# Fewer weight parts in the first five blocks, and the rest tied to the feed-forward steps at 0.85 a step

## The chip, the cores and the metric

The kernel is one program on 1 core of a Trainium2 chip. The metric is the device time of one execution in microseconds (us). The kernel before takes 1225.81 us, the median of 3 runs (1225.13 to 1226.35).

## The reference, cut to what matters

Three layers follow each other: linear attention with an exponential feature map, a feed-forward layer with a token shift and a gate, and a second feed-forward layer with a short convolution. The change touches the preparation of the weights of the second one (`w_k`, `w_r`, `w_v`).

```python
def _attn_ref(q, k, v, w_phi):            # batch 8, 8 heads, 576 tokens, head size 64, 128 features
    def phi(x):
        proj = np.einsum('bhsd,df->bhsf', x, w_phi)
        proj = proj - np.max(np.abs(proj), axis=-1, keepdims=True)
        return np.concatenate([np.exp(proj), np.exp(-proj)], axis=-1)
    q_p, k_p = (phi(q), phi(k))
    kv = np.einsum('bhsf,bhsd->bhfd', k_p, v)
    z = np.sum(k_p, axis=2)
    num = np.einsum('bhsf,bhfd->bhsd', q_p, kv)
    den = np.einsum('bhsf,bhf->bhs', q_p, z)[..., None] + 1e-06
    return num / den

def _moe_ref(x, mu_k, mu_r, w_k, w_v, w_r):    # d_model 512, d_ff 1024
    xk = mu_k * x + (1.0 - mu_k) * x_prev       # x_prev: x one token earlier
    xr = mu_r * x + (1.0 - mu_r) * x_prev
    k = np.maximum(xk @ w_k, 0.0)
    v = k * k @ w_v
    r = 1.0 / (1.0 + np.exp(-(xr @ w_r)))
    return r * v
```

## The kernel before, in words

Heads are worked in 32 pairs `Pi` (8 batches of 4 pairs). `block(Pi)` is the attention of several pairs at once: it turns the centred projections of pair `Pi` (`turn`, tiles `pt`, then `qf` through ScalarE's exponential), projects the keys of pair `Pi+2` (`front`, tiles `p` and `pk`), the queries of pair `Pi+1` (`pq`), sums keys against values for pair `Pi+1` (`sums4`, tile `pkv`) and gives the results of pair `Pi` (`results`, tile `pn`, normalised into `xn` by VectorE). `column` transposes a finished `xn` (tile `px`), and ScalarE copies it into `xT`, the input of the feed-forward layer. TensorE runs in the order in which the code is written (`manual_schedule`); the order on VectorE and ScalarE is fixed at build time by the framework's scheduler, and each engine runs its list in order.

Every projection ends in VectorE: a maximum (`mx`) and a subtraction (`t`) for each tile. The PSUM tiles of the attention come from five rotating buffers (`psa`), so `pk` of one block can only start when VectorE has read the `pn` tiles of the block before, and from block 5 on the second `pk` tile follows ScalarE's copy of `px`.

The feed-forward layer `moe(u)` runs over 16 half batches `u`. From pair 4 (`MS`) on, `feed` puts its steps behind the blocks: 6 steps behind block 4, 6 behind block 5, 7 behind block 6, 9 behind block 7, then 10. A step is one output tile: for `u` = 0 steps 0 to 7 are `psk`, 8 and 9 `psr`, 10 and 12 `psv`, 14 and 15 `psr`, 16 and 18 `psv`; the odd ones between are the reads of `psv`. The half batch `u` = 0 multiplies by the unsplit weights, the later ones by a high and a low half.

The three weights come as 64-bit numbers in 20 parts of 512 columns: 8 of `wk`, 2 of `wr`, 4 of `wv`, 2 of `wr`, 4 of `wv`. The generator `step` (L171 to L186) moves one part on: SP loads `raw` (512 KB, three buffers); ScalarE makes `h` from the upper words; VectorE builds a 32-bit number in `h` with four instructions (two `TENSOR_SCALAR`, two `SCALAR_TENSOR_TENSOR` that also read `raw`); SP stores `h` into the weight's tile (`wkl`, `wrh`, `wvl`), and `ready` counts up. `tick` (L209) loads a new part and finishes the part that was loaded two ticks earlier, so on SP's queue the load of part n+3 stands right behind the store of part n, whose `raw` buffer it takes. `pre` gives ScalarE its instruction early.

A tick stands in three sorts of places: twice in every block from -1 to 6; at the fixed steps of the table `WAT` behind blocks 4, 5 and 6; and in `want`, in front of a feed-forward step of `u` = 0, until `ready` is 2 (`AHEAD`) above the number of parts that this step reads (`needs`). A step of `u` = 1 then splits the parts (`split`: a copy on ScalarE, tile `wkh`, and a subtraction on VectorE, `wkl<-wkl,wkh`).

Of the kernel before, what the change touches and what calls it, by code (L numbers as in the profile page):

```python
# [27 lines left out]

MS, SLOW, SR = 4, 8, {4: 6, 5: 6, 6: 7, 7: 9}

WAT = {4: (4, 10), 5: (3, 7, 11), 6: (3, 5, 7, 9)}
DS0 = 10
AHEAD = 2
HS = S // 2
V1 = D + 1

# [6 lines left out]
def fused_kernel(ctx: ExitStack, tc: tile.TileContext, qk, va, wphi, ones2, mu, wk, wv, wr, win, wout, cw, out):  # L43
# [33 lines left out]
    def f(x):  # L77
        return x.bitcast(F32)
# [78 lines left out]
    with ExitStack() as p1:  # L157
# [30 lines left out]
        def split(n=None):  # L188

            while n is None or cleft[0] < n:  # L190
                if half:
                    hs, ls = half.pop()
                    V.behind("tensor_tensor", ls, f(ls), f(hs), ALU.subtract)
                    cleft[0] += 1
                if whole and (n is None or cleft[0] < n):
                    half.append(whole.pop(0))
                    A.behind("copy", half[0][0], f(half[0][1]))
                if n is None or not half:
                    return

        under, ready, whole, half, cleft = [], [0], [], [], [0]

        def pre():

            if under and under[0][1] == 2 and not under[0][2]:
                next(under[0][0])
                under[0][2] = True

        def tick():  # L209
            pre()  # L210
            new = [wsteps.pop(0), 0, False] if wsteps else None
            if new:
                next(new[0])
            if under and under[0][1] == 2:
                next(under.pop(0)[0], None)
            if new:
                under.append(new)
            for x in under:
                x[1] += 1

        wsteps = [step(wk, wkh, wkl, o) for o in range(0, 4096, 512)]
        for h in range(2):
            for w in ((wr, wrh, wrl), (wv, wvh, wvl)):
                n = w[1].shape[1] // 2
# [13 lines left out]
        def load(Pi):  # L238

            b, p = divmod(Pi, NP)  # L240
            raw = pool.tile([P, W], F32, tag="x", bufs=3, name="rqk")
            if Pi == 0:
                for c in (slice(KC0, W), slice(0, KC0)):
                    SY.dma_start(raw[:, c], qk[b, p, :, c])
            else:
                (SY if Pi < 3 else G).dma_start(raw, qk[b, p])
            xk[Pi] = raw
# [86 lines left out]
        def column_end(xn, xt, px):  # L334
            T.transpose(px[:, :P], xn[:, 4], ident)

            def copies():
                for h in range(2):
                    r = slice(64 * h, 64 * h + 64)
                    A.copy(xt[r, 513:577], px[r, r])  # L340
            return copies
# [46 lines left out]
        def block(Pi):  # L388

            nq, nk = Pi + 1 < B * NP, Pi + 2 < B * NP  # L390
            if 0 <= Pi < B * NP - 3:
                load(Pi + 3)
            if Pi >= 0:
                if Pi > MS:
                    x = column(Pi - 1)
                qf, t1 = turn(Pi)
                pr = psa.tile([P, 512], F32, tag="at", name="pr")
                if Pi > MS:
                    copies = column_end(*x, pr)
                turn_end(qf, t1, pr)  # L400
                if Pi > MS:
                    copies()
            pre()
            if nk:
                tk = front(Pi + 2)
            if -1 <= Pi < 7:
                tick()
            if 1 <= Pi <= MS:
                x = column(Pi - 1)
                column_end(*x, psm.tile([P, 512], F32, tag="mm", name="pr"))()  # L410
            if nq:
                ts[Pi + 1] += centre4(rows4(Pi + 1, 0, "pq"), "tq")
                del xk[Pi + 1]
                sums4(Pi + 1)
            if Pi >= 0:
                results(Pi, qf)
            pre()
            if nk:
                features(Pi + 2, tk)
                if Pi + 2 > 1:  # L420
                    load_v(Pi + 2)
            if -1 <= Pi < 7:
                tick()

        def attention(Pi):
# [39 lines left out]

        done = [0]

        def want(n):

            while ready[0] < min(n + AHEAD, 20):  # L470
                tick()
            due[0] += 1

        due = [0]
        needs = [*range(1, 9), 9, 10, 12, 14, 15, 16, 18, 20]

        def moe(u):
            b, hf = divmod(u, 2)
# [5 lines left out]
                    T.matmul(ps, f(wl), xh, start=first, stop=last)  # L484

            def need(n):
                want(n)
                if u:
                    split(n)

            def soon():
                if u == 0 and due[0] < len(needs) and ready[0] < min(needs[due[0]] + AHEAD, 20):
                    pre()
            o = hf * HS
            for j in range(2):
# [78 lines left out]
        load_v(1)  # L574

        def extras(Pi, n):
            if n in WAT.get(Pi, ()):
                tick()
            if n + 1 in WAT.get(Pi, ()):
                pre()  # L580
            if Pi == 7 and n == 14:
                taps()
            if Pi >= DS0 and dsteps and n in (3, 11):
                dsteps[0] = dsteps[0][0](), dsteps[0][1]
            if Pi >= DS0 and dsteps and n in (4, 12):
                raw, step = dsteps.pop(0)
                step(raw)
# [177 lines left out]
```

## Time and profile before

| | |
|---|---|
| median of 3 runs | 1225.81 us |
| the profiled execution, its own time | 1225.83 us |
| span of its trace | 1224.0 us |
| outside the span | 1.83 us |
| TensorE busy | 1202.0 us, 98% |
| VectorE busy | 762.1 us, 62% |
| ScalarE busy | 696.7 us, 57% |
| granted TensorE clock | 1.00, the upper level (2.4 GHz) throughout |

The busy shares are means over the whole span. The weights' parts are moved in its first 122 us, where the shares are others; the rows further down show that stretch. The profiled execution took within 0.02 us of the median, so a sum made against it stands against the median as well.

### The profile page before, as it was taken

The numbers are of one execution on the slowest core, as the hardware profiler recorded it, in microseconds if no ns is written. First come the engines' busy times: TensorE is split into PE (matmuls) and PEld (weight loads), VectorE is DVE, ScalarE is ACT, GpSimd is POOL, SyncE is SP. The second block draws the span as 40 slices with busy tenths as digits, with TensorE's granted clock in tenths as the row PEclk, the third lists the DMA queues.
The fourth block names the chain that finished last, engine by engine and source line by source line (L and its number), as shares of the span: only waits on it lengthen the run. The fifth ranks groups of instructions, "written<-read, shape, count | busy, mean of one in ns | idle before, by whom it ended". The sixth has DMA issues, their size and how long they took to land.

```text
span 1224.0 us, 29034 instructions
## 1 busy us (share of the span) xinstructions
PE 1202.0 (98%) x11920; PEld 1135.5 (93%) x11920; DVE 762.1 (62%) x1584; ACT 696.7 (57%) x1644; POOL 86.3 (7%) x213
## 2 busy tenths in 40 slices
PE   7899999999999999999999999999999999999998
PEld 6787999999999999999999999998889888888887
DVE  7989676576675765766656534426555754466555
ACT  6777765566565655665555533325654655455554
POOL 1000001111111111111000000000000000000000
PEclk9999999999999999999999999999999999999999
DMA  6665121223232322332110004050122101210220
GB/s 223 221 218 196 59 80 59 86 93 120 89 93 76 117 83 86 93 121 71 50 42 23 11 21 158 20 188 19 44 63 63 43 21 62 63 53 11 63 62 32
DMA packets 56532, 100.81 MB, mean 82 GB/s; under 512 B 10320, under 2 KB 38608, under 8 KB 56400
## 3 DMA queue, kind: packets, MB, share of 16 engines
q1 hardware_dynamic: 40272, 61.65, 14.8%
q0 software_dynamic: 6768, 27.69, 7.4%
q10 hardware_dynamic: 9360, 9.61, 2.8%
q8 instruction: 94, 1.54, 0.5%
q14 instruction: 38, 0.31, 0.1%
HBM read 66.42 MB, written 27.26 MB: 77 GB/s over the span
## 4 chain that ended last, share of the span: by engine, by line
PE 90%; DVE 5%; ACT 2%; issue 1%; DMA 1%; SPq 0%; ACTq 0%; DVEq 0%
PE psh L150 5%; PE psh L152 5%; PE psh L151 5%; PE psv L150 5%; PE pkv L318 5%; PE psv L151 5%; PE psk L151 5%; PE psv L152 5%; PE psk L152 5%; PE psk L150 5%; PE pso L150 5%; PE pso L151 5%; PE pso L152 5%; PE pn L371 4%; PE psr L150 3%; PE psr L151 3%
## 5 line engine op out<-in xcount | busy, mean ns | idle before, releaser
L58 DVE SCALAR_TENSOR_TENSOR ct<-h,cw,ct 128x460 f32<-128x460 f32 (+2 forms) x160 | 111.4, 696 | 84.6 <-ACT ct L58 83.5
L150 PE MATMUL psv<-kh,wvl 128*128 128x288 f32 x480 | 142.2, 297 | 0.0
L151 PE MATMUL psv<-kl,wvh 128*128 128x288 f32 x480 | 141.9, 296 | 0.0
L151 PE MATMUL psk<-ml,wkh 128*128 128x288 f32 x480 | 141.7, 295 | 0.0
L152 PE MATMUL psk<-mh,wkh 128*128 128x288 f32 x480 | 141.4, 295 | 0.0
L152 PE MATMUL psv<-kh,wvh 128*128 128x288 f32 x480 | 141.1, 294 | 0.0
L150 PE MATMUL psk<-mh,wkl 128*128 128x288 f32 x480 | 140.9, 294 | 0.0
L152 PE MATMUL psh<-xh,wih 128*128 128x462 f32 (+1 forms) x320 | 118.9, 372 | 0.0
L151 PE MATMUL psh<-xl,wih 128*128 128x462 f32 (+1 forms) x320 | 118.8, 372 | 0.0
L151 PE MATMUL pso<-gl,woh 128*128 128x460 f32 (+1 forms) x320 | 117.9, 370 | 0.0
L152 PE MATMUL pso<-gh,woh 128*128 128x460 f32 (+1 forms) x320 | 117.7, 370 | 0.0
L58 ACT ACTIVATE kf<-psk 128x288 f32<-128x288 f32 x128 | 52.2, 408 | 111.5 <-PE psk L152 105.6
L150 PE MATMUL psh<-xh,wil 128*128 128x462 f32 (+1 forms) x320 | 107.3, 372 | 0.0
L58 ACT ACTIVATE h<-psh 128x462 f32<-128x462 f32 (+3 forms) x128 | 47.8, 409 | 76.8 <-PE psh L152 75.6
L150 PEld LDWEIGHTS psv<-kh,wvl 128*128 128x128 f32 x480 | 90.3, 188 | 0.8
L151 PEld LDWEIGHTS psv<-kl,wvh 128*128 128x128 f32 x480 | 90.4, 188 | 0.0
L150 PEld LDWEIGHTS psk<-mh,wkl 128*128 128x128 f32 x480 | 90.2, 188 | 0.1
L151 PEld LDWEIGHTS psk<-ml,wkh 128*128 128x128 f32 x480 | 90.2, 188 | 0.0
L152 PEld LDWEIGHTS psv<-kh,wvh 128*128 128x128 f32 x480 | 90.2, 188 | 0.0
L152 PEld LDWEIGHTS psk<-mh,wkh 128*128 128x128 f32 x480 | 90.2, 188 | 0.0
L58 ACT ACTIVATE kp<-t 128x512 f32<-128x512 f32 x128 | 70.3, 618 | 34.6 <-PE pkv L318 28.9
L58 DVE SCALAR_TENSOR_TENSOR x<-sg,psv 128x288 f32<-128x288 f32 x64 | 29.0, 454 | 97.5 <-PE psv L152 91.4
(108 smaller groups left out, 2822.7 us busy)
## 6 DMA issues: line engine op xcount, KB each, us to landing
rqk<-qk POOLq DMA_DIRECT2D x29, 576.0 KB, 4.8
va<-va POOLq DMA_DIRECT2D x30, 325.0 KB, 4.8
x2s<-x SPq DMA_DIRECT2D x30, 288.0 KB, 2.3
raw<-wk SPq DMA_DIRECT2D x8, 512.0 KB, 5.4
raw<-wv SPq DMA_DIRECT2D x8, 512.0 KB, 4.0
raw<-win SPq DMA_DIRECT2D x16, 256.0 KB, 2.9
raw<-wout SPq DMA_DIRECT2D x16, 256.0 KB, 2.9
x2r<-x2s ACTq DMA_DIRECT2D x16, 231.0 KB, 2.6
```

The costliest lines, as they stand in the source:

```text
L58: x = op(*a, **k)
L150: T.matmul(ps, wl, xh, start=first, stop=False)
L151: T.matmul(ps, wh, xl, start=False, stop=False)
L152: T.matmul(ps, wh, xh, start=False, stop=last)
L318: T.matmul(o[r:r + 64], k_[:, r:r + 64], v_, start=(i == 0), stop=(i == len(prods) - 1))
L371: T.matmul(pn[b_][64 * r:64 * r + 64, j], qf[h_][:, c, o:o + 64], kv[:, c, h_], start=(j == 0 and c == 0), stop=(j == 4 - b_ and c == 1))
```

## The change

`WAT` and `AHEAD` go. In blocks 0 to 3 one tick stands in place of two, and in blocks 5 and 6 none (blocks -1 and 4 keep two). In front of each step of `u` = 0 that reads a part, `want` ticks until `ready` reaches a goal: 6 (`PRE`) parts and 0.85 (`RATE`) for each step so far, or the parts that the step reads if these are more.

```diff
-WAT = {4: (4, 10), 5: (3, 7, 11), 6: (3, 5, 7, 9)}
+PRE, RATE = 6, 0.85
 DS0 = 10
-AHEAD = 2
...
             pre()
             if nk:
                 tk = front(Pi + 2)
-            if -1 <= Pi < 7:
+            if -1 <= Pi <= MS:
                 tick()
...
-            if -1 <= Pi < 7:
+            if Pi in (-1, MS):
                 tick()
...
-        def want(n):
-
-            while ready[0] < min(n + AHEAD, 20):
+        needs = [*zip([*range(11), 12, 14, 15, 16, 18], [*range(1, 11), 12, 14, 15, 16, 18, 20])]
+
+        def goal():
+
+            at, n = needs[0]
+            return min(20, max(n, int(PRE + RATE * (at + 1))))
+
+        def want():
+
+            while ready[0] < goal():
                 tick()
-            due[0] += 1
-
-        due = [0]
-        needs = [*range(1, 9), 9, 10, 12, 14, 15, 16, 18, 20]
+            needs.pop(0)
...
             def need(n):
-                want(n)
                 if u:
                     split(n)
+                else:
+                    want()
 
             def soon():
-                if u == 0 and due[0] < len(needs) and ready[0] < min(needs[due[0]] + AHEAD, 20):
+                if u == 0 and needs and ready[0] < goal():
                     pre()
...
-            if n in WAT.get(Pi, ()):
-                tick()
-            if n + 1 in WAT.get(Pi, ()):
-                pre()
```

By these rules the parts that are done (`ready`) in the order of the program are, before and now: 10 and 6 behind block 4, 12 and 11 behind the steps after it, 14 and 11 behind block 5, 17 and 15 behind the steps after it, 19 and 15 behind block 6, 20 and 20 behind the steps after that.

The order on TensorE, SP and GpSimd is the same as before, instruction by instruction. VectorE and ScalarE do the same instructions in another order. Three places show how; `h` is always a weight part, and lines of the kernel now stand one lower (L58 is L57).

On VectorE, in each of blocks 1 to 4, behind the results `xn` of the pair before. Before:

```order
L58 TENSOR_SCALAR xn<-pn,rd 128x128
L58 TENSOR_SCALAR h<-h 128x512
L58 TENSOR_REDUCE mx<-p_1076 128x1
L58 TENSOR_REDUCE mx<-p_1077 128x1
L58 TENSOR_SCALAR h<-h 128x512
L58 TENSOR_TENSOR t<-p_1076,mx 128x128
L58 TENSOR_TENSOR t<-p_1077,mx 128x128
L58 SCALAR_TENSOR_TENSOR h<-raw,h 128x512
L58 TENSOR_REDUCE mx<-pk 128x4 x2
L58 SCALAR_TENSOR_TENSOR h<-raw,h 128x512
L58 TENSOR_TENSOR t<-pk,mx 128x512 x2
```

And now:

```order
L57 TENSOR_SCALAR xn<-pn,rd 128x128
L57 TENSOR_REDUCE mx<-p_1040 128x1
L57 TENSOR_REDUCE mx<-p_1041 128x1
L57 TENSOR_TENSOR t<-p_1040,mx 128x128
L57 TENSOR_TENSOR t<-p_1041,mx 128x128
L57 TENSOR_REDUCE mx<-pk 128x4 x2
L57 TENSOR_TENSOR t<-pk,mx 128x512 x2
```

One of the two parts of each of these blocks is gone from here; the other one, behind `t<-pk`, stays.

On ScalarE, from the last `psk` tiles of the steps behind block 4 into block 5 (`kf` is the read of a `psk` tile, `xT<-px` and `qf<-pt` belong to block 5). Before:

```order
L58 ACTIVATE h<-raw 128x512
L58 ACTIVATE kf<-psk 128x288
L58 ACTIVATE kh<-kf 128x576
L58 ACTIVATE kf<-psk 128x288 x2
L58 COPY xT<-px 128x512
L58 ACTIVATE kh<-kf 128x576
L58 ACTIVATE qf<-pt 128x512 x4
```

And now:

```order
L57 ACTIVATE h<-raw 128x512
L57 ACTIVATE kf<-psk 128x288
L57 ACTIVATE kh<-kf 128x576
L57 ACTIVATE kf<-psk 128x288
L57 ACTIVATE h<-raw 128x512
L57 ACTIVATE kf<-psk 128x288
L57 ACTIVATE h<-raw 128x512
L57 COPY xT<-px 128x512
L57 ACTIVATE kh<-kf 128x576
L57 ACTIVATE qf<-pt 128x512 x4
```

Two more parts (the 10th and the 11th) stand ahead of the copy `xT<-px`.

On VectorE, behind the results `xn` of block 6, in the steps that end `u` = 0. Before, up to the end of the last part:

```order
L58 TENSOR_SCALAR xn<-pn,rd 128x128
L58 TENSOR_SCALAR h<-h 128x512 x2
L58 SCALAR_TENSOR_TENSOR h<-raw,h 128x512 x2
L58 TENSOR_TENSOR wkl<-wkl,wkh 128x512
L58 TENSOR_SCALAR h<-h 128x512
L58 SCALAR_TENSOR_TENSOR x_1600<-sg,psv 128x288
L58 TENSOR_SCALAR h<-h 128x512
L58 SCALAR_TENSOR_TENSOR h<-raw,h 128x512 x2
```

And now, from the 18th part's last instruction to the end of the last part:

```order
L57 SCALAR_TENSOR_TENSOR h<-raw,h 128x512
L57 TENSOR_SCALAR h<-h 128x512
L57 TENSOR_TENSOR ml_1842<-xf,mh_1841 128x576
L57 TENSOR_SCALAR h<-h 128x512
L57 TENSOR_TENSOR ml_1842<-xf,mh_1841 128x576
L57 SCALAR_TENSOR_TENSOR h<-raw,h 128x512
L57 TENSOR_SCALAR h<-h 128x512
L57 SCALAR_TENSOR_TENSOR h<-raw,h 128x512
L57 TENSOR_SCALAR h<-h 128x512
L57 SCALAR_TENSOR_TENSOR h<-raw,h 128x512
L57 SCALAR_TENSOR_TENSOR x_1857<-sg,psv 128x288
L57 SCALAR_TENSOR_TENSOR h<-raw,h 128x512
```

Between `xn` of block 6 and the end of the last part stood two parts, one `wkl` and one `x`; now there stand five parts, three `wkl`, two `x` and two `ml` (one `wkl`, next to last, and the first three parts are not shown).

## Rows read from the trace of the kernel before

**Rows 1.** The page: busy time of TensorE; VectorE's busy tenths, 40 slices.

```profile
PE 1202.0 (98%) x11920; PEld 1135.5 (93%) x11920; DVE 762.1 (62%) x1584; ACT 696.7 (57%) x1644; POOL 86.3 (7%) x213
...
DVE  7989676576675765766656534426555754466555
```

**Rows 2.** Busy time of each engine in two stretches of the parts.

```profile
core 0: us, PE busy (x) PEld busy (x) DVE busy (x) ACT busy (x) POOL busy (x), PEclk, DMA share, GB/s
23.04:69.80 46.76, 38.74 (x803) 34.48 (x798) 46.45 (x113) 37.68 (x99) 4.29 (x8) 1.00 0.64 207
...
92.69:125.38 32.69, 31.33 (x289) 25.64 (x288) 31.94 (x68) 21.38 (x50) 2.20 (x7) 1.00 0.58 198
```

**Rows 3.** Waits of TensorE, 0 to 130 us: total, times, longest.

```profile
PE pk L261 <- DVE xn L58: 4.9, 4, 1.2
...
PE pt L350 <- DVE t L58: 3.4, 5, 0.9
...
PE psv L484 <- DVE x L58: 0.7, 1, 0.7
PE pn L371 <- DVE t L58: 0.7, 1, 0.7
```

**Rows 4.** Timeline of TensorE: start, duration, instructions, idle before and its releaser.

```profile
62.01 1.25 PE L261 MATMUL pk<-wp,rqk 64*128 64x128 f32 x16 [1.23 <-DVE xn L58]
...
69.53 11.91 PE L484 MATMUL psk<-mh,wkl 128*128 128x288 f32 x48
...
83.33 1.06 PE L261 MATMUL pk<-wp,rqk 64*128 64x128 f32 x16
...
119.62 8.03 PE L484 MATMUL psv<-kh,wvl 128*128 128x288 f32 x32 [0.70 <-DVE x L58]
127.49 0.60 PE L330 MATMUL px<-ident,xn 128*128 128x128 f32 x4
```

**Rows 5.** Timeline of VectorE, block 3 to the last part.

```profile
58.12 1.29 DVE L58 TENSOR_TENSOR t<-pq,mx 128x512 f32<-128x512 f32 x2
...
62.03 0.42 DVE L58 TENSOR_SCALAR h<-h 128x512 f32<-128x512 f32 x1
...
64.09 1.29 DVE L58 TENSOR_REDUCE mx<-pk 128x4 f32<-128x512 f32 x2
...
69.80 1.29 DVE L58 TENSOR_TENSOR t<-pq,mx 128x512 f32<-128x512 f32 x2
...
73.71 0.88 DVE L58 TENSOR_SCALAR h<-h 128x512 f32<-128x512 f32 x2
...
83.53 0.49 DVE L58 TENSOR_REDUCE mx<-p 128x1 f32<-128x128 f32 x2 [3.23 <-PE p L261]
...
92.69 0.88 DVE L58 TENSOR_SCALAR h<-h 128x512 f32<-128x512 f32 x2
...
115.93 0.88 DVE L58 TENSOR_SCALAR h<-h 128x512 f32<-128x512 f32 x2
116.85 1.42 DVE L58 SCALAR_TENSOR_TENSOR h<-raw,h 128x512 uint32<-128x512 uint32 x2
...
119.94 1.42 DVE L58 SCALAR_TENSOR_TENSOR h<-raw,h 128x512 uint32<-128x512 uint32 x2
```

**Rows 6.** Timeline of SP: a load, and the stores of parts 13 and 18.

```profile
73.02 0.90 SPq L174 DMA_DIRECT2D raw<-wv  x1
...
91.36 0.47 SPq L184 DMA_DIRECT2D wvl<-h  x1
...
114.67 0.47 SPq L184 DMA_DIRECT2D wvl<-h  x1
```

**Rows 7.** Tile `raw`, 23 to 114 us: its loads, issue to landing.

```profile
DMA to landing us min/median/max: 3.6/4.1/6.4
```

**Rows 8.** Tile `wvl`, 60 to 125 us: its stores, issue to landing.

```profile
DMA to landing us min/median/max: 2.3/2.3/4.9
```

**Rows 9.** Timeline of ScalarE: a part that waited for its load.

```profile
77.05 0.68 ACT L58 ACTIVATE h<-raw 128x512 f32<-128x512 f32 x1 [0.97 <-DMA raw<-wv]
```

## The prediction

> **What bounds the kernel now.** I read the page first, then the stretches, the waits, and the timelines of single engines. The page's shares [rows 1] name TensorE, busy for 98% of the span; but VectorE's tenths begin at 7 to 9 and fall only behind the fifth slice, so the start has another limit than the mean. The stretches show it: from 23.04 to 69.80 us, blocks 0 to 3, VectorE is busy for 46.45 of 46.76 us and TensorE for 38.74; from 92.69 to 125.38 VectorE is busy for 31.94 of 32.69 us [rows 2]. In the first stretch VectorE sets the pace and TensorE waits for it: `pk` for `xn`, 4.9 us in 4 times, and `pt` for `t`, 3.4 us in 5 [rows 3]. In the second one TensorE is nearly full as well, with two waits for VectorE of 0.7 us. All 20 parts of the weights are VectorE's work in these two stretches and between. The only slack of note that VectorE has there is the 3.23 us in front of block 5 [rows 5].
>
> **What is removed.** One block to the next is 69.80 − 58.12 = 11.68 us, from `t<-pq` to `t<-pq` [rows 5]. One part leaves each of blocks 1 to 4: two instructions between `xn` and the maximum of `pk`, one between the two, one ahead of `t<-pk`. Its four instructions are 2 × 0.42 + 1.42 = 2.26 us long [rows 5], the upper bound of what a block can gain. Not all of it comes back, since the maximum needs `pk`. `pk` starts at 62.01 and lasts 1.25, so it ends at 63.26 [rows 4]; the maximum starts at 64.09 [rows 5]. Ahead of it 0.83 us can go, the lower bound if no more is gained; the instruction between the maximum and `t<-pk` gives another 0.60 (1.42 for two, less their overlap). The part that stays now has its last two instructions next to each other, some 0.05 us dearer. I take 0.83 + 0.60 − 0.05 = 1.4 a block, since `pk` itself moves with `xn` and the next block repeats the pattern.
>
> TensorE's `pk` of block 4 comes behind three such blocks: 62.01 − 4.2 = 57.8, and the first `psk` 69.53 − 4.2 = 65.3 [rows 4]. VectorE has gained four times by the end of block 4: 73.71 − 5.6 = 68.1 [rows 5].
>
> **What is added, and where it lands.** The four parts come back later, beside other parts that move. I follow VectorE to the end of part 20 and count what it still has to do. A part in one piece takes 116.85 + 1.42 − 115.93 = 2.34, less 0.09 of overlap with what follows: 2.25 us [rows 5].
>
> *Behind block 4.* Parts 6 and 7 are loaded early; they take twice 2.25 less 0.25, since their instructions stand in turns, to 72.3, and part 8 another 2.25, to 74.6. Now the three `raw` buffers count. Part 9's load stands behind the store of part 6 (done at 70.5) and goes out some 0.6 later, as the load that was issued at 73.02 did behind its store, at 71.15 [rows 6]. Loads land 3.6 to 6.4 us behind their issue, 4.1 in the median [rows 7], so part 9 is there at 75.2, ScalarE takes 0.65, and VectorE waits from 74.6 to 75.85: 1.25 us. In the kernel before, ScalarE once waited 0.97 us for such a load in this very place [rows 9]. Parts 9 and 10 then end at 80.4, with part 10's load just in time. Block 5 begins with part 11 among its projections, as it had one part before; it took 92.69 − 83.53 = 9.16 us, and I take 9.0. So `xn` of block 5 is through at 89.4 in place of 92.69, 3.3 us earlier, but with 11 parts done where the store at 91.36 was the 13th [rows 6]. Two parts are 4.5 us: VectorE is 1.2 us behind. The 3.23 us of slack are used up.
>
> *Steps behind block 5, and block 6.* This stretch took 115.93 − 92.69 = 23.24 us with five parts (the store at 114.67 is the 18th [rows 6]). Now it has four: 23.24 − 2.0 = 21.25 (2.0 lies between 2.25 for a part in one piece and 1.86 for one spread among others, 2.26 less four overlaps of 0.1). `xn` of block 6 is through at 110.65, 5.3 us earlier and three parts behind.
>
> *Steps behind block 6.* From 115.93 the last two parts, one `wkl` and one `x` took until 119.94 + 1.42 = 121.36, less the overlap 121.28: 5.35 us [rows 5]. Now there are three more parts (6.3), one more `x` (0.36), two more `wkl` (1.2) and two `ml` (1.33 less 0.1): 5.35 + 9.1 = 14.4 us. Part 20 ends at 125.05, 3.8 us later than before.
>
> **What TensorE makes of it.** The store of part 20 lands 2.3 us later [rows 8], at 127.4; before at 123.65, when the second half of the last `psv`, which reads it, began at 119.62 + 6 = 125.5, with 1.9 us to spare [rows 4]. That half takes 127.49 − 125.5 = 2.0 us. So block 7 starts at 127.4 + 2.0 = 129.4 where it started at 127.49: **+1.9 us**. On the way TensorE gives back its 4.2 us in pieces: in block 5 the second `pk` waits for the copy `xT<-px`, which now stands on ScalarE behind the 11th part (its load lands at about 79.5, the copy ends at 80.7, `pk` could start at 79.1), and `pq` for `qf` behind it, 2.1 us together; `pq` of block 6 some 0.9 us behind the 16th part in the same way; then the `psv` tiles for parts 17, 19 and 20, some 4.5 us. From block 7 on, order and work are the same and TensorE was the bound, so the 1.9 us stay. The sum: 1225.83 + 1.9 = **1227.7 us**, against the profiled execution's own time, which stands 0.02 us from the median.
>
> The landing of part 9 is the term that a page prices otherwise. By the Trainium skill, DMA: Bandwidth & Descriptors, section Anatomy of one DMA, a transfer costs about 2.0 us plus its bytes over 436 GB/s, an estimate of 3.2 us for 512 KB; the sum by it would be 1226.8. Rows 7 are nearer to the case: none landed under 3.6.
>
> Bounds: the gain of a block 0.83 to 2.26, thus VectorE at 68.1 between 70.4 and 64.7, of which the early side helps little, as the loads hang on the stores; the landing of the load 3.6 to 6.4 (−0.5 to +2.3 on VectorE), twice in a row for parts 8 and 11; the store's landing 2.3 to 4.9.
>
> **The rivals.**
>
> *The gain stays (faster).* If VectorE had room behind block 4, no part would come late. TensorE then runs from 57.8 without a stop: 127.49 − 62.01 less its two waits of 0.7 is 64.1, block 7 at 121.9, 5.6 us earlier, 1220.2; with the 2.1 us of block 5, 1222.3. It needs part 20 by 121, 4 us before my sum. For it: 98% for TensorE [rows 1], and VectorE's 3.23 us in front of block 5. Against it: no other slack in [rows 2]. The Trainium skill, Perfetto Trace Analysis, section Identifying the Most-Contended Engine, has one optimise the engine with the highest occupancy, which is TensorE here by its weight loads too (93%); by that rule each wait taken from TensorE would be kept, 1225.83 − 4.2 = 1221.6. The same page's remark on several regimes is what [rows 2] bear out.
>
> *Loads are late (clearly slower).* Behind block 4 each load waits for a store and each part for a load. If parts 8 and 11 land at 6.4 in place of 4.2, as one did, VectorE is 3.8 us later at block 5 and block 7 moves to +5.7: 1231.5; at half of that, 1229.6. It decides from about 0.5 us of extra landing. For it: the kernel before had landings that long [rows 7]. Against it: half of its loads landed within 4.1.
>
> *Nearly even.* VectorE keeps one to two of its lost microseconds, say in cheaper parts or a wait less for part 9: 1224.0 to 1225.7.
>
> **How the numbers follow.** A time within 0.2%, 2.45 us, of the time before is about what a measurement cannot tell from no change. My forecast, 1225.8 to 1229.0, has 0.47; the gain stays 0.17; loads are late 0.26; nearly even 0.10. Faster by over 0.2% (under 1223.4) is most of the second: 0.15. Slower (over 1228.3) is the third and a quarter of the first: 0.37. Same: 0.48. For the range I leave about 0.1 at either end: 1222.5, inside the kept gain, to 1230.5, inside the late loads; the likeliest case has 1225.8 to 1229.0 of its own.
>
> **What the profile would show.** Right: blocks 1 to 3 at 10.3 us each, the first `psk` at 65.3; VectorE busy nearly without a gap from 68 to 125, but for a wait of about 1 us for a load; a wait of `pk` in block 5 for ScalarE's `xT`; waits of `psv` for stores of `wvl` between 113 and 128, where there was none; block 7 at 129.4. Wrong: `psk` later than 66.5 (the blocks gain less), or no wait of `psv` for a store (VectorE had room), or block 7 before 126.

## The result

The changed kernel took 1234.45 us in the median of six executions (1231.13 to 1235.37), the kernel before 1225.82 us (1225.13 to 1226.69): a ratio of 1.0067 with a 95% interval from 1.0054 to 1.0080. It is slower, by 8.6 us, where the prediction had 1.9 us and a range that ended at 1230.5. In a second comparison, on another occasion, it took 1232.36 us, ratio 1.0052 (1.0035 to 1.0068). The profiled execution is the shortest of the first six: its own time is 1231.13 us, its span 1229.4. So 5.3 of the 8.6 us stand in the trace of after, and 3.3 lie between that execution and the median.

The page's shares say nothing of it: TensorE's busy time has grown by 0.9 us and VectorE's by 1.3 [rows 1].

```profile
PE 1202.9 (98%) x11920; PEld 1135.5 (92%) x11920; DVE 763.4 (62%) x1584; ACT 696.5 (57%) x1644; POOL 88.1 (7%) x213
...
DVE  7999576576765765767646534426555754576555
```

The waits of TensorE, up to 135 us (waiter, line, what it waited for; total, times, longest), answer to [rows 3]:

```profile
PE psv L487 <- DMA wvl<-h: 5.2, 4, 1.8
...
PE pk L260 <- DVE xn L57: 4.1, 4, 1.2
PE pk L260 <- ACT xT L57: 2.0, 1, 2.0
...
PE pq L260 <- ACT qf L57: 1.5, 2, 1.1
PE pt L349 <- DVE t L57: 0.6, 2, 0.4
PE psr L487 <- DMA wrh<-h: 0.6, 1, 0.6
```

The waits of `pt` have shrunk from 3.4 to 0.6 us and those of `pk` for `xn` from 4.9 to 4.1, which is most of the gain. New are 5.2 us of `psv` and 0.6 of `psr` for stores of parts, 2.0 of `pk` for ScalarE's `xT` and 1.5 of `pq` for `qf`. TensorE's timeline (start, duration, instructions, idle before and its releaser) puts places to them, beside [rows 4]:

```profile
65.17 7.06 PE L487 MATMUL psk<-mh,wkl 128*128 128x288 f32 x28
...
81.30 1.16 PE L260 MATMUL pk<-wp,rqk 64*128 64x128 f32 x14 [1.95 <-ACT xT L57]
...
104.47 1.16 PE L260 MATMUL pq<-wp,rqk 64*128 64x128 f32 x16 [1.10 <-ACT qf L57]
...
120.50 2.18 PE L487 MATMUL psv<-kh,wvl 128*128 128x288 f32 x8 [1.56 <-DMA wvl<-h]
124.46 2.21 PE L487 MATMUL psv<-kh,wvl 128*128 128x288 f32 x8 [1.78 <-DMA wvl<-h]
127.94 2.18 PE L487 MATMUL psv<-kh,wvl 128*128 128x288 f32 x8 [1.27 <-DMA wvl<-h]
130.75 2.21 PE L487 MATMUL psv<-kh,wvl 128*128 128x288 f32 x8 [0.64 <-DMA wvl<-h]
132.80 0.60 PE L329 MATMUL px<-ident,xn 128*128 128x128 f32 x4
```

The first `psk` comes 4.36 us earlier than before, block 7 (`px` at 132.80) 5.31 us later. From there the two traces run alike, and the spans differ by 5.4. VectorE's timeline shows the way from the one to the other, beside [rows 5]:

```profile
53.70 1.28 DVE L57 TENSOR_TENSOR t<-pq,mx 128x512 f32<-128x512 f32 x2
63.92 1.28 DVE L57 TENSOR_TENSOR t<-pq,mx 128x512 f32<-128x512 f32 x2
67.89 0.88 DVE L57 TENSOR_SCALAR h<-h 128x512 f32<-128x512 f32 x2
...
75.78 0.89 DVE L57 TENSOR_SCALAR h<-h 128x512 f32<-128x512 f32 x2 [1.31 <-ACT h L57]
78.92 0.89 DVE L57 TENSOR_SCALAR h<-h 128x512 f32<-128x512 f32 x2 [0.79 <-ACT h L57]
...
90.07 0.88 DVE L57 TENSOR_SCALAR h<-h 128x512 f32<-128x512 f32 x2
...
98.85 1.10 DVE L57 TENSOR_SCALAR h<-h 128x512 f32<-128x512 f32 x3 [0.85 <-ACT h L57]
111.97 0.88 DVE L57 TENSOR_SCALAR h<-h 128x512 f32<-128x512 f32 x2
...
124.29 0.43 DVE L57 TENSOR_SCALAR h<-h 128x512 f32<-128x512 f32 x1 [1.31 <-ACT h L57]
...
127.68 0.69 DVE L57 SCALAR_TENSOR_TENSOR h<-raw,h 128x512 uint32<-128x512 uint32 x1
```

A block takes 63.92 − 53.70 = 10.22 us in place of 11.68, and VectorE has block 4 behind it at 67.89. Then it stops four times for ScalarE's `h`, 4.26 us in all, where the kernel before had none from 64 to 130 us. The last instruction of part 20 ends at 127.68 + 0.69 = 128.37; before it was 121.36 [rows 5].

Behind ScalarE's `h` stand the loads. In all four cases `h` had waited for the landing of its part's load: part 9 (4.0 us from issue to landing), part 10 (5.3), part 15 (4.7) and part 20 (5.1). Its timeline in block 5, beside [rows 9], and the landing of `raw`'s loads from 64 to 100 us, beside [rows 7]:

```profile
75.08 0.67 ACT L57 ACTIVATE h<-raw 128x512 f32<-128x512 f32 x1 [2.56 <-DMA raw<-wr]
...
80.11 0.66 ACT L57 ACTIVATE h<-raw 128x512 f32<-128x512 f32 x1 [0.93 <-DVE h L57]
80.68 0.57 ACT L57 COPY xT<-px 128x512 f32<-128x512 f32 x1
```

```profile
DMA to landing us min/median/max: 3.8/4.7/8.0
```

ScalarE waits 2.56 us for the load of part 9 and then, since it is behind, has part 11's `h` ahead of the copy `xT<-px` for which `pk` waits. At 80.11, as for part 10, the profile names VectorE as the releaser, but part 11's load, issued at 75.06, landed 5.0 us later, at 80.06: that wait was for a load too.

### The profile page after: what moved, and what is told of

It reads as the page before. It is cut to its first block, busy times and chain, and to the rows that moved or that the text cites. A ratio compares the mean times of both kernels' runs of the same rounds, so it can differ in the third digit from the quotient of the medians.

```text
span 1229.4 us, 29043 instructions
## 1 busy us (share of the span) xinstructions
PE 1202.9 (98%) x11920; PEld 1135.5 (92%) x11920; DVE 763.4 (62%) x1584; ACT 696.5 (57%) x1644; POOL 88.1 (7%) x213
## 4 chain that ended last, share of the span: by engine, by line
PE 89%; DVE 5%; ACT 2%; DMA 2%; issue 2%; SPq 0%; ACTq 0%; DVEq 0%
PE psh L151 5%; PE psh L149 5%; PE psh L150 5%; PE pkv L317 5%; PE psv L149 5%; PE psv L150 5%; PE psk L150 5%; PE psv L151 5%; PE psk L151 5%; PE psk L149 5%; PE pso L149 5%; PE pso L150 5%; PE pso L151 5%; PE pn L370 4%; PE psr L149 3%; PE psr L150 3%
## 5 line engine op out<-in xcount | busy, mean ns | idle before, releaser
L57 DVE SCALAR_TENSOR_TENSOR ct<-h,cw,ct 128x460 f32<-128x460 f32 (+2 forms) x160 | 111.5, 697 | 84.9 <-ACT ct L57 83.8
L57 ACT ACTIVATE kf<-psk 128x288 f32<-128x288 f32 x128 | 52.3, 408 | 109.3 <-PE psk L151 105.5
L57 ACT ACTIVATE h<-psh 128x462 f32<-128x462 f32 (+3 forms) x128 | 47.9, 410 | 77.0 <-PE psh L151 75.8
L57 DVE SCALAR_TENSOR_TENSOR x<-sg,psv 128x288 f32<-128x288 f32 x64 | 29.1, 454 | 99.0 <-PE psv L151 91.3
L57 ACT ACTIVATE kp<-t 128x512 f32<-128x512 f32 x128 | 70.3, 617 | 32.7 <-PE pkv L317 30.4
```

Of the source, the lines that this page charges most:

```text
L57: x = op(*a, **k)
```

## The experiments

All kernels below compute all of the reference. Each diff is against the changed kernel, if nothing else is said. Two numbers go with most of them: the start of the first `psk` (65.17 in after, 69.53 before) and that of `px` of block 7 (132.80 and 127.49). The kernel before took 1226.22 us beside the first four; 1226.13 beside the filled waits, the last steps behind block 7, one part fewer and the clamp; 1225.98 beside the catch-up, the four `raw` buffers, the kernel before with its last steps moved, and blocks 2 and 3; 1225.88 beside the three `tmps` buffers, blocks 0 and 1, and block 0 alone.

### The changed kernel again, and its parts

**The same kernel, to see a second profile.**

> The changed kernel once more, unchanged. Late parts (the account of its trace: TensorE waits for the stores of parts 16 to 20 between 116 and 131 us and for ScalarE in blocks 5 and 6): block 7 begins 5.3 us later than before, which gives 1231.1, as the traced execution had it. Clock: most executions take 3.3 us more, 1234.4, with a mean granted clock of 0.997; if that is TensorE's clock falling to its lower level for some us, a traced execution of 1234 shows a stretch below 1.00 somewhere behind the waits, and its waits up to 132 us are the same. Rival: the 3.3 us are longer waits (loads that land later); then a trace of 1234 shows block 7 at 136 and a clock of 1.00 throughout.

Measured: 1232.36 us (1231.37 to 1233.53); `psk` at 64.99, `px` of block 7 at 134.59. VectorE stopped 4.4 us for `h`, as in after. What differs is TensorE's clock. Its windows of 1 us (length; busy time and instructions of TensorE, its weight loads, VectorE, ScalarE, GpSimd; granted clock; share and GB/s of the DMA engines) show it behind the wait of `pk`, 2.16 us here against 1.95 in the first profile:

```profile
79.00:80.00 1.00, 0.17 (x2) 0.00 (x0) 0.93 (x3) 0.19 (x1) 0.00 (x0) 1.00 0.77 291
80.00:81.00 1.00, 0.00 (x0) 0.00 (x0) 0.97 (x2) 0.85 (x2) 0.00 (x0) 0.95 0.86 225
81.00:82.00 1.00, 0.66 (x6) 0.66 (x8) 1.00 (x4) 1.00 (x3) 0.00 (x0) 0.50 0.70 287
82.00:83.00 1.00, 1.00 (x13) 1.00 (x12) 1.00 (x4) 1.00 (x3) 0.00 (x0) 0.50 0.65 254
83.00:84.00 1.00, 1.00 (x11) 1.00 (x12) 1.00 (x4) 1.00 (x6) 0.00 (x0) 0.50 0.94 238
84.00:85.00 1.00, 1.00 (x19) 0.88 (x18) 1.00 (x2) 0.96 (x6) 0.00 (x0) 0.84 0.85 320
```

The granted clock is 0.50, the lower of its two levels, 1.2 and not 2.4 GHz, for some 3.4 us, from the end of the idle stretch on; in the first profile it stayed at 1.00 there. In block 5 that cost TensorE about 1.2 us beyond its waits, and VectorE waited 0.62 us for `pn`. Block 7 is 1.8 us later than in the first profile, but most of that has another source. VectorE's last instruction of part 20 and the last wait of TensorE are:

```profile
128.12 0.68 DVE L57 SCALAR_TENSOR_TENSOR h<-raw,h 128x512 uint32<-128x512 uint32 x1
132.55 2.21 PE L487 MATMUL psv<-kh,wvl 128*128 128x288 f32 x8 [1.71 <-DMA wvl<-h]
```

Part 20 was done at 128.80, 0.4 us later than in the first profile, and its store landed 3.7 us behind its issue, where the first had 2.3: 0.4 of the 1.8 us are VectorE's, 1.4 the store's.

**The blocks alone**, with the fixed places and the lead of two parts as before. The kernel is the one before with the second piece left out of blocks 0 to 3:

```
-            if -1 <= Pi < 7:
+            if Pi == -1 or 4 <= Pi < 7:
                 tick()
```

> Only the first half of the change: one tick in place of two in blocks 0 to 3, all else (table of fixed steps, two ticks in blocks 4 to 6, two parts ahead) as before. Late parts: the first psk at 65.2 as with the whole change; behind block 4 VectorE has only 3 parts to do in place of 5 and idles some 4 us before block 5, so the last part ends later than with the whole change, near 128 to 130, and block 7 begins at 132 to 135: 1230 to 1234 us without a fall of the clock. If the goal rule were what costs, this kernel would keep the saving: 1220 to 1222.

Measured: 1234.89 us (1234.38 to 1235.43), ratio 1.0073 (1.0058 to 1.0088); `psk` at 65.58, block 7 at 136.41. The gain is there and so is the loss: VectorE stands idle for 3.7 us in front of block 5, since the fixed places ask for two parts only, and the parts are late from then on. Two waits of `psv` are followed by the lower clock:

```profile
98.91 5.81 PE L484 MATMUL psv<-kh,wvl 128*128 128x288 f32 x16 [2.90 <-DMA wvl<-h]
114.35 4.15 PE L484 MATMUL psv<-kh,wvl 128*128 128x288 f32 x16
```

The same sixteen instructions take 5.81 us behind a wait of 2.90, and 4.15 without one: 1.7 us for a fall of the clock. The expectation had no such fall in it; two of them, 3.3 us, lie in the profiled execution, and if both pass on in full, its block 7 would stand at about 133.1 without them, inside the 132 to 135 that were expected.

**The goal rule alone**, with two parts a block as before:

```
-            if -1 <= Pi <= MS:
+            if -1 <= Pi < 7:
                 tick()
...
-            if Pi in (-1, MS):
+            if -1 <= Pi < 7:
                 tick()
```

> Only the second half: blocks as before (two ticks in -1 to 6), the table and the two parts ahead replaced by 6 parts and 0.85 a step. Late parts: 10 parts are done by block 4, so the goal asks for little; the end of part 20 moves by 0 to 2 us, within the room of 1.9 us that it has: 1225.5 to 1228. If the goal rule were what costs: 1230 or more.

Measured: 1231.06 us (1230.67 to 1231.19), ratio 1.0042 (1.0027 to 1.0057); block 7 at 132.87. The expectation missed by 3 us. With ten parts done the rule asks for no part until the steps have come up to it, and VectorE stands idle:

```profile
80.84 0.89 DVE L57 TENSOR_SCALAR h<-h 128x512 f32<-128x512 f32 x2 [4.50 <-ACT h L57]
83.83 0.49 DVE L57 TENSOR_REDUCE mx<-p 128x1 f32<-128x128 f32 x2 [0.65 <-PE p L260]
```

So 12 and not 13 parts stand ahead of the `xn` of block 5, and 16 and not 18 ahead of that of block 6. Either half alone costs 5 to 9 us, by the same route: VectorE's room in front of block 5 goes unused and the parts come late.

**Two parts a block again in blocks 5 and 6:**

```
-            if -1 <= Pi <= MS:
+            if -1 <= Pi < 7:
                 tick()
...
-            if Pi in (-1, MS):
+            if Pi == -1 or MS <= Pi < 7:
                 tick()
```

> The change with the two ticks of blocks 5 and 6 put back, so that three parts and not five stand behind the results of block 6. Late parts: VectorE's whole work up to part 20 is the same and it is full, so the end of part 20 moves little, 125 to 128, and the total is 1228 to 1231. Rival, it is the heap of five parts at the end that costs: then 1222 to 1225, as the earlier parts lie beside TensorE's work.

Measured: 1230.44 us (1229.71 to 1231.44), block 7 at 131.54, as expected. 12 and 16 parts stand ahead of the `xn` of blocks 5 and 6; one more each than in the changed kernel, at a gain of 1.9 us against it in the same comparison, and the waits of `psv` stay (0.8 to 1.6 us each). Its profile too has a stretch of 0.50 in block 5, behind a wait of `pk` of 2.18 us.

### The clock, and the place of the last steps

**Work for TensorE while it waits.** The `p` products of block 5 are written five times over, and products that nobody reads stand ahead of the late halves of `psv`:

```
+            for _ in range(5 if Pi == MS + 3 else 1):
                 rows(Pi, [(ps[h][:, 0], h, 4) for h in range(2)])
...
+                        if u == 0 and mp and kc in (0, FC // 2):
+                            for _ in range(1 if j and kc else 3):
+                                T.matmul(full[:, HS:], f(wkl[:, :P]), k2[0][0][:, 0, :512 - HS], ...)
```

> The changed kernel, with TensorE given idle work where it waited: the four `p` products of block 5 are written five times in place of once (the same values again), and ahead of the `psv` tiles that wait for parts 17 to 20 it multiplies into columns that nobody reads (three, three, three and one products). Nothing else changes, so work for VectorE, loads and stores stay as they are. Theory (granted clock): the part of the loss that the profiled waits don't hold, 1234.4 against 1231.1 in the first comparison, is TensorE at 0.50 of its clock behind idle stretches of 2 us and more; without such a stretch no window from 78 to 136 us shows 0.50, all executions lie at 1229 to 1231.5 with a mean clock of 0.999 or 1.0. Rival (the clock is a by-product): the median stays where the changed kernel's was, 1232.4 to 1234.5, with the same spread.

Measured: 1230.49 us (1229.93 to 1231.5), ratio 1.0039 (1.0026 to 1.0051). All five executions lie in the stretch that was expected, and none is at 1234 or over, as most of the changed kernel's first six were. TensorE does more and the kernel is 1.9 to 4.0 us shorter than the changed kernel in its two comparisons. Two things keep this from being clean. Two executions still had a mean clock of 0.998, and they were not the longer ones (1230.18 and 1230.49; the three at 1.000 took 1229.93, 1231.28 and 1231.50). And in the profiled one VectorE's stops for `h` were 3.1 and not 4.3 us, for which the edit gives no reason; block 7 is 1.3 us earlier there than in the changed kernel's first profile, about that difference.

**The last two `psv` steps behind block 7**, and not ahead of it:

```
-MS, SLOW, SR = 4, 8, {4: 6, 5: 6, 6: 7, 7: 9}
+MS, SLOW, SR = 4, 8, {4: 6, 5: 6, 6: 4, 7: 12}
...
                 mix_next(u + 1, mp)
+                if u == 0 and mp:
+                    yield
```

> The changed kernel, with the last two `psv` steps of the first half, which read parts 17 to 20, behind block 7 and not ahead of it. VectorE's order of the parts stays but for part 20. Theory (the parts come late at the end): the four waits of `psv` for stores, 5.3 us in the profile after, mostly go, since TensorE has block 7 in between; block 7 itself waits a little for VectorE; 3 to 5 us less than the changed kernel, 1226.5 to 1229.5, with the `pk` wait of block 5 for `xT` still there. Rival (VectorE is the bound through block 7 as well, so that the wait only moves into block 7): 1230 or more.

Measured: 1228.42 us (1226.75 to 1230.28), ratio 1.0020 (1.0011 to 1.0029). The 5.2 us of `psv` for stores are down to 0.8, and TensorE has block 7 in between; so the late parts were a loss mostly because of where the steps that read them stood. The eleven executions also order themselves by the mean granted clock: four at 1.000 took 1226.75, 1226.81, 1226.92 and 1227.53, three at 0.998 took 1228.24, 1228.42 and 1228.60, four at 0.996 to 0.997 took 1229.61, 1229.62, 1229.80 and 1230.28. From group to group that is 1.4 us. The profiled one, at 0.998, has one stretch of 0.50, from about 81.5 to 84.8 us, at the end of this wait and behind it:

```profile
81.75 1.86 PE L260 MATMUL pk<-wp,rqk 64*128 64x128 f32 x13 [2.28 <-ACT xT L57]
```

**One part fewer behind block 4** (`PRE, RATE = 5, 0.85`), on top of that:

> As the kernel with the last two `psv` steps behind block 7, and PRE is 5 and not 6, so that one part fewer is asked for behind block 4. Theory (late loads hold up ScalarE, which holds up `xT` and so `pk`): the `pk` wait for `xT` in block 5, 2.0 to 2.2 us, shrinks to under 1 us, the granted clock stays at 1.0 there, and the time is 1.5 to 3 us under that of the kernel with PRE 6: 1224 to 1227. Rival (the wait of `pk` is covered, as the part comes back later): the same time as with PRE 6.

Measured: 1235.17 us (1234.57 to 1235.63), ratio 1.0074 (1.0062 to 1.0087). Both theories missed. The wait of `pk` for `xT` shrank to 0.5 us as expected, but every part is asked for one step later, so parts are late that were in time: `psr` waits 2.06 and 1.75 us, `psv` 1.58 us ahead of block 6 and 2.06 behind block 7. A part saved in one place was lost in four. Of the two waits of 2.06 us the second is followed by a clock of 0.50, the first by 1.00.

**The same, caught up behind block 5** (PRE 5 for the six steps behind block 4, then 6):

> As the kernel with the last two `psv` steps behind block 7, but PRE is 5 for the six steps behind block 4 alone and 6 from there on, so 10 parts and not 11 stand ahead of the `xn` of block 5, and 15 again ahead of that of block 6. Theory: the wait of `pk` for `xT`, 2.3 us, and the granted clock of 0.50 behind it go, and no part is late behind block 5: 1224.5 to 1226.5, with a mean clock of 1.0. Rival (one part later behind block 4 is one part later at the end, as with PRE 5): `psr` and `psv` wait 2 us or more, 1228 to 1233.

Measured: 1227.64 us (1226.86 to 1228.21), ratio 1.0013 (1.0004 to 1.0022). No execution has a mean clock under 0.999, and no wait of `pk` for `xT` is over 0.5 us; but a part is late for `psr`, which waits 1.82 us, and so the time lies 1.1 us over the expected range, which ended at 1226.5, and the kernel does not beat the one before.

**The clamp on GpSimd**, the first of the four instructions of a part:

```
-            V.behind("tensor_scalar", h, h, 2.0 ** -31, 122879.9921875 * 2.0 ** -16, ALU.max, ALU.min)
+            G.behind("tensor_scalar", h, h, 2.0 ** -31, 122879.9921875 * 2.0 ** -16, ALU.max, ALU.min)
```

> The changed kernel, with the first of the four instructions of each part, the clamp of `h`, on GpSimd and not on VectorE. VectorE has 20 times 0.42 us less, 8.4 us, about 5 of it behind block 4; GpSimd took 1.2 us for a TENSOR_SCALAR of 128x256 in the kernel before. Theory (VectorE's place in the queue makes the parts late): the waits of `psv` for stores shrink by 2 us or more, 1226 to 1230. Rival (the loads set the pace behind block 4, VectorE is only behind them): the parts wait as before and GpSimd's longer instruction is added to each: 1231 to 1235.

Measured: 1235.62 us (1234.18 to 1237.9). It tells nothing about VectorE's share, as the remedy is worse than the load: the instruction takes GpSimd 1981 ns, where VectorE had 0.42 us, and VectorE then stops for it. Groups of instructions up to 140 us, and VectorE's waits from 60 to 140:

```profile
L57 POOL TENSOR_SCALAR h<-h 128x512 f32<-128x512 f32 x20 | 39.5, 1981 | 31.6 <-ACT h L57 29.7 <-DVE rd L57 1.8
```

```profile
DVE h L57 <- POOL h L57: 9.8, 8, 2.3
```

### The loads

**Four `raw` buffers**, in all three places that name them, and each load a tick earlier, for which block -1 has a third tick, so that the plan of the parts stays; `tmps` has three buffers and not four, which makes the room:

```
-TMPS = 4
+TMPS = 3
...
-            raw = pool.tile([P, 512, 2], U32, tag="raw", bufs=3, name="raw")
+            raw = pool.tile([P, 512, 2], U32, tag="raw", bufs=4, name="raw")
...
-            if under and under[0][1] == 2:
+            if under and under[0][1] == 3:
...
             if -1 <= Pi <= MS:
+                tick()
+            if Pi == -1:
                 tick()
```

> The changed kernel with four `raw` buffers in place of three, each load a tick earlier, and `tmps` with three buffers in place of four to make room. The plan of parts stays: 5, 11, 15 and 20 parts ahead of the `xn` of blocks 4 to 7. Theory (late loads took what was not in my sum): VectorE's waits for ScalarE's `h`, 1.31, 0.79 and 0.85 us up to block 6 and 1.31 behind it, go, `pk` of block 5 no longer waits 2 us for `xT`, the `psv` waits shrink by 2 to 4 us; `px` of block 7 at 128.5 to 130.5 in place of 132.8; 1227 to 1230, if three `tmps` buffers cost nothing. Rival (VectorE's work by itself makes the parts late): the waits for loads go but the `psv` waits stay within 1 us of their 5.3; `px` of block 7 at 132 or later.

**Three `tmps` buffers and nothing else**, the control for it:

> The changed kernel with three `tmps` buffers in place of four and nothing else: the control for the run with four `raw` buffers. If late loads cost what that run suggests, `px` of block 7 stands here at 132 to 135 as in the changed kernel, against 129.2 there, with VectorE's waits for `h` back; and the stretch from there to the end is about 2 us longer than in the changed kernel, so 1232 to 1237. If the fourth `raw` buffer did nothing and the three `tmps` buffers made the difference, `px` of block 7 is at 130 or earlier.

Measured: 1229.70 us (1229.12 to 1232.57) with four `raw` buffers, 1234.61 (1233.52 to 1237.02) with three and the same `tmps`. The first `psk` stands at 64.27 and 64.21, block 7 at 129.20 and 133.13. From block 7 to the end of the span they take 1098.7 and 1098.6 us, 2.0 more than the changed kernel, which is the price of the missing `tmps` buffer; what the loads cost lies ahead of block 7, 3.9 us of it. That includes a fall of the clock in the control, which waited 2.53 us for `xT`; the changed kernel's first profile, without a fall, took 67.6 us from `psk` to block 7, where four buffers take 64.9: 2.7 us without a fall in either. VectorE's waits from 64 to 130 us, first of the run with four (its 5.1 us for `psv` come behind the last part):

```profile
DVE x L57 <- PE psv L489: 5.1, 1, 5.1
DVE rd L57 <- PE pn L370: 0.4, 1, 0.4
DVE h L57 <- ACT h L57: 0.2, 1, 0.2
```

```profile
DVE h L57 <- ACT h L57: 3.6, 4, 1.4
DVE rd L57 <- PE pn L370: 1.5, 3, 0.8
```

The loads land no sooner (3.7/4.4/6.4 us, shortest, median and longest, with four buffers, 3.7/4.1/5.9 in the control); they are issued sooner, that of part 9 at 66.22 and not at 70.06. With the stops for `h` gone, VectorE goes from the `xn` of block 4 to its last part in 55.4 us (67.06 to 122.43, start of its last instruction), where after took 59.7 (67.97 to 127.68): 4.3 us, and 4.3 was the sum of after's stops. One point was missed: the waits of `psv` and `psr` for parts did not shrink, 6.1 us together. TensorE comes to them 2.4 us earlier, because the waits of `pk` and `pq` are down from 3.45 to 1.03 us, and meets the same parts earlier; and the store of part 20, done on VectorE at 123.12, landed 4.0 us behind its issue, 2.3 in after:

```profile
122.43 0.69 DVE L57 SCALAR_TENSOR_TENSOR h<-raw,h 128x512 uint32<-128x512 uint32 x1
...
127.15 2.21 PE L489 MATMUL psv<-kh,wvl 128*128 128x288 f32 x8 [1.96 <-DMA wvl<-h]
```

### How much the early blocks can give

**The kernel before with the last two `psv` steps behind block 7**, as a control:

> The kernel before, with the last two `psv` steps of the first half behind block 7 and nothing else changed. It is the control for the others that move these steps: before has no wait of `psv` for a store, so moving them should give nothing, 1225.3 to 1226.9. If it is faster by 1 us or more, the steps' place is a gain by itself, and the other kernels' times are to be read against this one.

Measured: 1225.80 us (1225.14 to 1226.69), ratio 1.0000 (0.9991 to 1.0009). Where no `psv` waits for a store, the place of the steps gives nothing, as expected.

**One part less in two blocks, one more behind block 4**, on that (against the kernel before):

```
-WAT = {4: (4, 10), 5: (3, 7, 11), 6: (3, 5, 7, 9)}
+WAT = {4: (2, 6, 10), 5: (3, 7, 11), 6: (3, 5, 7, 9)}
...
-            if -1 <= Pi < 7:
+            if -1 <= Pi < 7 and Pi not in (2, 3):
                 tick()
```

> The kernel before, with one piece less in blocks 2 and 3 alone, a third fixed place behind block 4 (2, 6, 10 in place of 4, 10), and the last two `psv` steps of the first half behind block 7: 7, 12, 17 and 20 parts ahead of the `xn` of blocks 4 to 7, where before had 9, 13, 18 and 20. Theory (blocks gain 1.4 us each, and VectorE's 3.23 us in front of block 5 hold one part and no more): the first `psk` at 66.7, no wait of VectorE of over 0.5 us in front of block 5, block 7 without a wait for a store: 1223 to 1225. Rival (one part behind is enough to make TensorE wait for stores): 1226 to 1229.

Measured: 1227.12 us (1225.42 to 1228.61), ratio 1.0010 (1.0001 to 1.0018): missed by 2 us. `psk` stands at 68.50 and not at 66.7, since a part that leaves block 3 does so behind the `pk` that `psk` follows; only one of the two gains lies ahead of it (and the work began 1.0 us later in this execution, by the first `xn`, than in the control). And in block 7 a wait of 1.42 us for `xT` is followed by a stretch of clock 0.50.

**The same with blocks 0 and 1 in place of 2 and 3:**

> As the kernel with one piece less in two blocks, with these in blocks 0 and 1 and not 2 and 3, so that both gains of 1.4 us lie ahead of the first `psk`: `psk` at 66.7 to 67.2, and 7, 12, 17 and 20 parts ahead of `xn` of blocks 4 to 7 as there. Theory (TensorE keeps what VectorE has room to pay for): block 7 begins 1.4 us earlier than there, 1224 to 1226. Rival (parts 9 to 12 wait for their loads, ScalarE's copies stand behind them, and TensorE's granted clock falls behind the wait): 1226.5 to 1229.

Measured: 1225.30 us (1224.42 to 1227.61), ratio 0.9996 (0.9987 to 1.0005). `psk` at 65.85, block 7 at 115.69, 2.6 us ahead of the control (0.2 of it an earlier start). Against the kernel before 0.6 us of that is left, which the interval does not tell from nothing. The wait of 1.42 us in block 7, 0.27 in the control, is there again, and the windows from its end on read:

```profile
119.00:120.00 1.00, 0.11 (x2) 0.12 (x4) 0.93 (x3) 1.00 (x3) 0.00 (x0) 1.00 1.04 318
120.00:121.00 1.00, 1.00 (x15) 1.00 (x16) 1.00 (x2) 1.00 (x3) 0.00 (x0) 0.82 0.43 162
121.00:122.00 1.00, 1.00 (x12) 1.00 (x13) 1.00 (x3) 1.00 (x6) 0.00 (x0) 0.50 0.28 111
122.00:123.00 1.00, 1.00 (x12) 0.78 (x10) 1.00 (x4) 0.47 (x5) 0.00 (x0) 0.50 0.95 270
123.00:124.00 1.00, 1.00 (x21) 1.00 (x22) 1.00 (x4) 0.00 (x0) 0.57 (x1) 0.50 0.38 143
```

**One part less in block 0 alone** (`and Pi != 0`, the third place behind block 4 kept, all else as in the kernel before):

> The kernel before with one piece less in block 0 alone and a third fixed place behind block 4 (2, 6, 10): 8, 13, 18 and 20 parts ahead of `xn` of blocks 4 to 7, so that no part is later behind block 5 than in the kernel before. Theory: VectorE's 3.23 us in front of block 5 hold the one part of 2.25 us, the 1.4 us are kept: 1224 to 1225. Rival (the extra load behind block 4 is late, and the wait takes the 1.4 us back): 1225.5 to 1227.

Measured: 1224.88 us (1223.8 to 1225.7) against 1225.88 (1224.76 to 1227.53), ratio 0.9991 (0.9983 to 1.0000). The first `psk` is at 68.20, 1.3 us earlier, block 7 at 126.58, 0.9 us earlier. VectorE's wait in front of block 5 shows where the part went:

```profile
DVE mx L58 <- PE p L261: 1.6, 1, 1.6
DVE h L58 <- ACT h L58: 1.2, 2, 0.9
```

The 3.23 us of [rows 5] are 1.6 now. This is the one version whose gain on the kernel before, 1.0 us, reaches the edge of what the measurement can tell.

## Why the prediction was wrong

*The gain of a block held.* Predicted 1.4 us a block, measured 11.68 − 10.22 = 1.46; the first `psk` at 65.3, measured 65.17; VectorE behind block 4 at 68.1, measured 67.89.

*The route of the loss held.* The wait of `pk` in block 5 for `xT` behind the 11th part, the wait of `pq` for `qf` and those of `psv` for parts 17 to 20 are all in the trace, and the run with the last steps behind block 7 shows that the last ones cost what they seem to: without them 3.9 us fewer than in the changed kernel's second comparison.

*The step that failed is the wait for loads, in size.* The prediction followed the loads to one stop of 1.25 us for part 9 and took each later load to be just in time. After stopped four times, 4.3 us. The first stop came as priced (1.31 us; the load went out at 71.02 and landed in 4.0 us, predicted 71.15 and 4.1). The other three, for parts 10, 15 and 20, were not in the sum: 2.95 us. Followed along VectorE: `xn` of block 5 through at 90.07 (predicted 89.4), of block 6 at 111.97 (110.65), part 20 done at 128.37 (125.05). These 3.3 us pass on to block 7, 132.80 against 129.4.

The run with loads in time bears VectorE's part of the sum out: with four `raw` buffers the stops are gone but for 0.2 us, and VectorE needs 56.1 us from the `xn` of block 4 to the end of part 20, where the prediction had 57.0 from 68.1 to 125.05, of which 1.25 were the stop. That block 7 stood at 129.20 there, predicted 129.4, is luck: part 20 was done at 123.1 and not 125.05, its store took 4.0 us to land and not 2.3, and the first `psk` was 0.9 us earlier than in after.

So the rival with late loads, at 0.26 and 1229.6 to 1231.5, was the case in kind, and it holds the profiled execution, though not the median; but the parts that it named were not the late ones (part 8 landed in 3.8 us, part 11 in 5.0). Loads landed in 4.7 us in the median, where I had taken 4.1. That row was the wrong one: 4.1 is the median of all loads from 23 to 114 us, and the change moves loads to where they follow each other closely. In the kernel before the loads that went out at 78.64 and 80.89, each about 2 us behind another, had landed in 5.2 and 5.1 us; the four of after from 72.81 to 81.85 landed in 4.7 to 5.3. What lengthens them, their closeness or the other traffic there, no run separates.

By the Trainium skill, DMA: Bandwidth & Descriptors, section Anatomy of one DMA, the estimate for such a load was 3.2 us; that section gives its figures for transfers that GpSimd issues, and these loads are SP's. No load of after from 64 to 100 us was under 3.8, and the measurement decides.

*A term that was missing is TensorE's clock, and its share is shown only in part.* No term of the sum and no rival had it, as the trace of before shows no fall. The new waits bring it: 0.50 for about 3.4 us, 1.2 to 1.7 us of TensorE's time each, seen in the second profile of the changed kernel and in those of eight experiments. The median of the first comparison stands 3.3 us above its profiled execution, and four of the five longer executions have a mean clock of 0.997, as the blocks alone had in the profile with two falls. For the clock speak the run with filled waits, whose five executions all lie under 1231.6, and the steps of 1.4 us in the run with the last steps behind block 7. Against the clock as the whole of it speaks the second profile of the changed kernel: there 1.4 of the 1.8 us by which block 7 came later are a longer landing of part 20's store. So landings, the rival in the expectation of that run, have a share too. No execution at 1234 was profiled, one of them had a mean clock of 0.999, and how the 3.3 us divide stays open.

*The rival of a kept gain* rested on TensorE's 98% (93% by its weight loads), and on the Trainium skill, Perfetto Trace Analysis, section Identifying the Most-Contended Engine: the engine with the highest occupancy is the one to relieve. TensorE was relieved of 4.4 us and all of it was given back 55 us later; the stretches of [rows 2] were the better guide.

The sum as it came out: 1225.8 + 1.9 as predicted, + 3.4 for loads that were later than predicted (block 7 at 132.80 and not 129.4), + 3.3 between the profiled execution and the median, of the clock and of landings in shares that stay open: 1234.4.

## What to carry to other kernels

Work that is taken off a full engine has to be followed to the place where it is done instead, along with the loads that bring its data: with three buffers a load can go out only behind the store that frees its buffer, so parts that bunch up wait for their loads, 0.8 to 1.3 us each here, however free the engine is. Price such a load by the loads of the stretch into which it moves, and not by the median of all. Move only as much as the slack ahead holds: one part into 3.2 us of slack gained 1.0 us, four parts lost 8.6. And price a new idle stretch of TensorE of two microseconds at more than its length, since the work behind it may run at half the clock for a while.

## What the hardware showed that was not expected

The granted clock of TensorE fell to its lower level behind short stops: in the first 200 us of the profiles here behind ten waits of 2.02 to 2.90 us, and in block 7 of two runs behind one of 1.42 us. The length of the wait alone does not decide it: the clock stayed at 1.00 behind 1.95 us in the first profile of the changed kernel, behind one of 2.06 us in the run with one part fewer, and behind 2.71 us in the run with the clamp on GpSimd. Each time it stayed at 0.50 for about 3.4 us, through work that filled the engine. In the run with the last steps behind block 7 the executions differ by steps of 1.4 us that go with the mean clock.

The same store of 256 KB, that of part 20, landed 2.3 us behind its issue in the first profile of the changed kernel, 3.7 in the second and 4.0 in the run with four `raw` buffers; where TensorE waited for it, block 7 moved with it.

GpSimd took 1.98 us for a TENSOR_SCALAR of 128x512 that takes VectorE 0.42.
